# Joining the two first products of every table multiplication, two more groups of idle matmuls and a new order of work, in a fused S4 convolution and GLU kernel

## The chip, the cores and the metric

The kernel runs on one core of a Trainium2 chip. The metric is the device time of one execution in microseconds; for the kernel before it is the median of three runs. A separate execution was recorded by the hardware profiler, and every row that is shown comes from it.

## What is computed

The input x has 2048 tokens of 512 channels. It is normalised over the channels without learned parameters (xn). Two branches read xn, and the output is the input plus both of them.

```
K   = einsum("dn,dnl,dn->dl", Cc, exp(dt*A*l), dt*Bc).real      # 128 complex modes a channel
y   = irfft(rfft(xn, 4096) * rfft(K, 4096))[:2048] + xn*Dskip    # a causal convolution a channel
glu = (sigmoid(xn @ w_gate) * (xn @ w_up)) @ w_down              # 512 -> 1792 -> 512
out = x + y + glu
```

## The kernel before

**The plan.** The kernel first describes its work as 979 steps. `pl.add` names a step's engine, its modelled cost, the steps that it depends on and the slots of buffer pools that it takes and gives back. The list `ORDER` then fixes the sequence in which all steps are emitted, so it fixes the order on every engine and on every queue of transfers. Each engine works through its own steps strictly in that order. Slots are given out in the order of `ORDER` too: a pool with fewer buffers forces a later step behind the one that frees a buffer. Lists of step numbers choose engines: `ON_DVE` (which copies run on VectorE, the others run on ScalarE), `ON_ACT` (whose layer norm statistics ScalarE takes) and `UEV` (for which units of the GLU the up projection is first copied out of PSUM by ScalarE).

**The GLU branch.** There are four groups of 512 tokens (g0 to g3), and 14 blocks of 128 hidden channels in each. One block is a gate projection (L1027, four matmuls of 512 columns), a sigmoid on ScalarE (L1036), an up projection (L1042, four matmuls), and a product on VectorE (L1057). For a unit in `UEV` ScalarE first copies the up projection into `us_sb` (L1053), and the product reads that; otherwise the product reads PSUM directly. The down projection (L1086) takes 14 matmuls for each 128 tokens. Matmul groups land in eight PSUM banks, which the pool `b` hands out.

**The convolution branch.** It is a transform along tokens, a product with the transform of K, and the transform back:

- The tokens are transformed in pairs of tiles (`fx2`, L680), copied out of PSUM and stored to `z_scr` in DRAM.
- The powers of exp(dt*A) are made by a ladder of eleven squarings (L652 on ScalarE, L661 and L663 on VectorE). Each rung is cast into the tables `W` by a DMA that GpSimd issues (L657).
- For each of four blocks of 128 channels (c = 0 to 3) two tables are built: G with 16 columns and H with 41 columns of complex numbers. Columns that are rungs are copied in from `W` (the "seeds", by `pl.copy`). The others come from `cmul`, a complex multiplication of n columns by one rung, and from `squares` (L771 on ScalarE, L776 and L777 on VectorE).
- `cmul` is two steps. Its step `f_a` forms two products on VectorE: L718 writes the columns times the real part of the rung into the table, L719 writes the columns times the imaginary part into a temporary buffer. Its step `f_b` then combines them with two more instructions (L723, L724). A block has ten such multiplications, of n = 1, 1, 2, 2, 4, 4, 4, 4, 7 and 8 columns; n columns are 256 n elements a partition for L718 and for L719, and 128 n for L723 and L724. The temporary buffer has two slots (the pool `tg`).
- When G and H of a block are done, TensorE multiplies them (`f_k`, L802, two halves of 64 small matmuls). ScalarE or VectorE copies the result out, `f_sel` (L823, L827) sorts it, and two copies leave it in `kT`.
- Four pairs of frequency units then run for each of two channel halves, blocks 0 and 1 first: loads from `z_scr` and of a constant E, the transform `fm` (L870), the kernel's transform `fk` (L886), products on VectorE (L891, L895, L902, L903), the transform `fv` or `fvs` (L919, L931) and a store. At the end L995 transforms back, and L1010 and L1106 add.

**G and H in memory.** G has two buffers, chosen by the parity of c, so the steps of G for block c wait for the matmuls of block c-2 (`gdep`). H has one, so the steps of H for block c wait for the matmuls of block c-1 (`hdep`):

```
G = at(OFF["G"] + 8 * KB * (c % 2), [NPR, 2, NGE, 2])
H = at(OFF["H"], [NPR, 2, NH, 2])
gdep = kgen.get(c - 2, [])
hdep = kgen.get(c - 1, [])
```

**The start.** TensorE begins with groups of idle matmuls on zeros (`keep_warm`, L516): one of nine and, by `WARM`, two of two. They share its order with the transposes of the first four normalised tiles (L561).

Of the kernel before, what the change touches and what calls it, by code (L numbers as in the profile page):

```python
# [10 lines left out]
BF = mybir.dt.bfloat16  # L11
# [18 lines left out]
CW = 128  # L30
# [19 lines left out]
WARM = (2, 2)  # L50
# [132 lines left out]
def _consts():  # L183
# [22 lines left out]
UEV = (5, 7, 8, 12, 13, 14, 16, 17, 19, 20, 21, 24, 25, 26, 27, 28, 30, 31, 32, 33, 34, 35, 36, 37, 38, 39, 40, 41, 43, 44, 46, 50, 51, 52, 53, 54,)  # L206
ON_DVE = (93, 94, 95, 107, 116, 191, 192, 367, 373, 486, 492, 501, 548, 590, 595, 598, 879,)
ON_ACT = (2, 8, 10, 11, 12,)
ORDER = [
# [114 lines left out]
def kernel(  # L324
# [21 lines left out]
    pl = _Plan(dict(b=NBK, hT=NHT, zs=4, zx=2, xx=4, es=3, kb=2, pp=2, vs=2, ot=3, tg=2, us=2, sq=2))  # L346
# [27 lines left out]
    us_sb = const.tile([128, 2, 512], BF, name="us_sb")  # L374
# [9 lines left out]
    NBIG = 118272  # L384
# [16 lines left out]
    for nm, sz in [("W1", 12 * KB), ("gc", 2 * KB), ("G", 16 * KB), ("H", 20992), ("tmp", 4 * KB), ("W0", 12 * KB),  # L401
                   ("xn", 16 * KB), ("lad", 16 * KB), ("kx", 8 * KB), ("zs", 4 * KB), ("pq", 2 * KB)]:
        OFF[nm] = o
        o += sz
# [4 lines left out]
    W = [at(OFF["W%d" % p], [12, 2, DW]) for p in range(NP)]  # L409
# [211 lines left out]
    wt = [at(o_, [NP, 2, DW], F32) for o_ in (lad0, lad0 + 4 * KB, lad0 + 8 * KB, OFF["kx"])]  # L621

    def f_w0():
        wd = lambda n: pt_[n].rearrange("p (w d) -> p w d", w=NP)
        V.tensor_tensor(out=wt[0][:, :, 0], in0=wd("rr"), in1=wd("sh"), op=ALU.mult)
        V.tensor_tensor(out=wt[0][:, :, 1], in0=wd("rr"), in1=wd("sn"), op=ALU.mult)
# [22 lines left out]
    for k in range(12):  # L649
# [5 lines left out]
        def f_cw(cur=cur, k=k):  # L655
            for p in range(NP):
                P.dma_start(out=W[p][:, k], in_=cur[:, p])  # L657
# [47 lines left out]
    TMP = dict(tg=[OFF["tmp"], OFF["lad"] + 12 * KB])  # L705

    def cmul(lo, outp, n, m, conj, buf, deps, prio):

        ne = n * NPR * 4
        wide = lambda v: v.rearrange("p r c k h -> p r c (k h)")  # L710
        mre = m[:, 0, :].rearrange("p (r h) -> p r h", h=2).unsqueeze(2).to_broadcast([128, NPR, 2 * n, 2])
        mim = m[:, 1, :].rearrange("p (r h) -> p r h", h=2).unsqueeze(2).to_broadcast([128, NPR, 2 * n, 2])
        sl = _Slot(buf)
        tb = lambda: at(TMP[buf][sl.idx], [2048])[:, 0:ne].rearrange(
            "p (r c k h) -> p r c k h", r=NPR, c=2, h=2)

        def f_a():
            V.tensor_tensor(out=wide(outp), in0=wide(lo), in1=mre, op=ALU.mult)  # L718
            V.tensor_tensor(out=wide(tb()), in0=wide(lo), in1=mim, op=ALU.mult)  # L719

        def f_b():
# [461 lines left out]
```

## Time and profile before

| what | value |
|---|---|
| median of 3 runs | 215.97 us (215.88 to 215.99) |
| the profiled execution | 216.53 us |
| its span, first to last instruction | 214.7 us |
| around the span | 1.83 us |
| instructions | 5758 |

The profile's page gives the busy time of each engine, a picture of the span in 40 slices, the chain of work that ended last, and groups of instructions by line. The views of the trace add stretches of time, waits by releaser, and single instructions in order of time. PE is TensorE, PEld its weight loads, DVE is VectorE, ACT is ScalarE, POOL is GpSimd. A duration runs from an instruction's start to its end; on TensorE and VectorE the next one often starts before that end, so the distance from start to start, called the interval here, is what an instruction costs its engine.

### The profile page before, as it was taken

What the parts mean: (1) busy time and instruction counts of PE and PEld (TensorE: products, weight loads), DVE (VectorE), ACT (ScalarE), POOL (GpSimd) and SP (SyncE); (2) the same over time, 40 slices, a digit from 0 to 9 for tenths busy, and PEclk for the clock granted to TensorE, in tenths of its full rate; (3) what the DMA queues carried; (4) which work ended last, traced back from release to release, by engine and by line L of the source; (5) the groups of instructions that cost most, each with busy time, mean ns of one, the idle gap of its engine ahead of it and who ended that gap; (6) DMA issues with size and microseconds to landing.
All of it is one profiled execution on the core that took longest, in us unless ns stands there. A gap on an engine that the chain in (4) does not pass through costs nothing.

```text
span 214.7 us, 5758 instructions
## 1 busy us (share of the span) xinstructions
PE 203.3 (95%) x2235; PEld 103.2 (48%) x2263; DVE 196.1 (91%) x425; ACT 175.8 (82%) x358; POOL 32.3 (15%) x66
## 2 busy tenths in 40 slices
PE   7799999999999999999999899999989999999993
PEld 2464443444444454445565464645635555444352
DVE  3899999999999999999999999999789989975682
ACT  3899999999999999888999999965569999825000
POOL 4229051351101400000000005000011000000200
PEclk9999999999999999999999999999999999999999
DMA  6999949665976857347544739716957997768843
GB/s 189 391 419 437 253 121 183 99 130 84 291 187 139 173 196 195 116 150 254 162 147 138 195 65 272 162 53 137 269 111 174 312 288 226 231 179 235 231 160 138
DMA packets 41613, 42.37 MB, mean 197 GB/s; under 512 B 8809, under 2 KB 35058, under 8 KB 41458
## 3 DMA queue, kind: packets, MB, share of 16 engines
q1 hardware_dynamic: 36642, 36.95, 54.8%
q0 software_dynamic: 4512, 4.73, 14.5%
q8 instruction: 18, 0.29, 0.6%
q10 hardware_dynamic: 432, 0.33, 0.5%
q14 instruction: 9, 0.07, 0.1%
HBM read 25.21 MB, written 12.07 MB: 174 GB/s over the span
## 4 chain that ended last, share of the span: by engine, by line
PE 48%; DVE 35%; ACT 9%; issue 3%; DMA 2%; SPq 0%; DVEq 0%; ACTq 0%
PE bank L1086 16%; PE bank L1042 9%; PE bank L1027 8%; PE bank L886 6%; DVE hT_sb L1057 5%; DVE big L719 5%; ACT big L293 5%; DVE big L718 5%; DVE big L723 3%; DVE big L724 3%; DVE big L600 3%; DMA big<-in_A_par_dram 2%; DVE stats L538 2%; PE bank L919 2%; PE bank L931 2%
## 5 line engine op out<-in xcount | busy, mean ns | idle before, releaser
L293 ACT ACTIVATE big<-bank 128x512 bf16<-128x512 f32 (+2 forms) x146 | 81.6, 660 | 8.7 <-PE bank L802 3.0
L1027 PE MATMUL bank<-xnT,wg_sb 128*128 128x512 bf16 (+1 forms) x230 | 52.6, 361 | 1.5 <-ACT us_sb L1053 0.3
L1042 PE MATMUL bank<-xnT,wu_sb 128*128 128x512 bf16 x216 | 52.3, 379 | 0.7 <-issue 0.2
L1086 PE MATMUL bank<-wd_sb,hT_sb 128*128 128x512 bf16 (+1 forms) x232 | 50.1, 367 | 1.6 <-issue 0.9
L1086 PEld LDWEIGHTS <-hT_sb 128*128 128x128 bf16 x238 | 22.5, 98 | 27.4 <-issue 3.8
L1036 ACT ACTIVATE hT_sb<-bank 128x512 bf16<-128x512 f32 x56 | 34.9, 671 | 0.3 <-PE bank L1027 0.2
L1027 PEld LDWEIGHTS <-wg_sb 128*128 128x128 bf16 x244 | 22.7, 98 | 23.3 <-issue 3.7
L1042 PEld LDWEIGHTS <-wu_sb 128*128 128x128 bf16 x224 | 21.2, 98 | 26.3 <-issue 2.3
L718 DVE TENSOR_TENSOR big<-big 128x1024 bf16<-128x1024 bf16 (+4 forms) x40 | 26.5, 664 | 0.2
L1053 ACT ACTIVATE us_sb<-bank 128x512 bf16<-128x512 f32 x36 | 23.6, 702 | 3.6 <-PE bank L1042 3.6
L719 DVE TENSOR_TENSOR big<-big 128x1024 bf16<-128x1024 bf16 (+4 forms) x40 | 26.3, 658 | 0.0
L891 DVE TENSOR_TENSOR big<-big 128x2048 bf16<-128x2048 bf16 x16 | 19.4, 1214 | 0.7 <-ACT big L293 0.5
L886 PE MATMUL bank<-big 128*128 128x256 bf16 x160 | 19.8, 273 | 0.0
L886 PEld LDWEIGHTS <-big 128*128 128x128 bf16 x160 | 15.3, 98 | 5.5 <-issue 2.0
L293 ACT ACTIVATE big<-big 128x256 bf16<-128x256 bf16 x34 | 17.7, 538 | 0.2 <-PE bank L802 0.2
L657 POOL DMA_DIRECT2D big<-big x24 | 13.1, 549 | 27.5 <-DVE big L663 15.2
L771 ACT ACTIVATE sq_sb<-big 128x256 bf16<-128x256 bf16 (+2 forms) x20 | 14.5, 740 | 2.4 <-DVE big L724 1.4
L723 DVE TENSOR_TENSOR big<-big 128x512 bf16<-128x512 bf16 (+4 forms) x40 | 16.3, 408 | 0.0
L724 DVE TENSOR_TENSOR big<-big 128x512 bf16<-128x512 bf16 (+4 forms) x40 | 16.3, 408 | 0.0
L1057 DVE TENSOR_TENSOR hT_sb<-hT_sb,us_sb 128x512 bf16<-128x512 bf16 x36 | 14.6, 414 | 1.3 <-ACT us_sb L1053 1.2
L1057 DVE TENSOR_TENSOR hT_sb<-hT_sb,bank 128x512 bf16<-128x512 bf16 x20 | 13.4, 680 | 0.2 <-PE bank L1042 0.2
L652 ACT ACTIVATE big<-big 128x1024 f32<-128x1024 f32 x11 | 12.2, 1112 | 0.2 <-DVE big L663 0.2
(98 smaller groups left out, 208.6 us busy)
## 6 DMA issues: line engine op xcount, KB each, us to landing
big<-c_E SPq DMA_DIRECT2D x16, 320.0 KB, 4.0
z_scr<-big SPq DMA_DIRECT2D x16, 256.0 KB, 3.0
big<-z_scr SPq DMA_DIRECT2D x16, 256.0 KB, 4.2
v_scr<-big SPq DMA_DIRECT2D x16, 256.0 KB, 3.1
big<-big POOLq DMA_DIRECT2D x24, 128.0 KB, 3.0
big<-in_A_u_dram SPq DMA_DIRECT2D x4, 512.0 KB, 13.0
big<-v_scr SPq DMA_DIRECT2D x4, 512.0 KB, 5.0
wu_sb<-in_B_w_up_dram SPq DMA_DIRECT2D x2, 896.0 KB, 11.8
```

The source lines that it names most:

```text
L293: nc.scalar.activation(out=get(out), in_=get(in_), func=ACT.Identity)
L718: V.tensor_tensor(out=wide(outp), in0=wide(lo), in1=mre, op=ALU.mult)
L719: V.tensor_tensor(out=wide(tb()), in0=wide(lo), in1=mim, op=ALU.mult)
L723: V.tensor_tensor(out=outp[:, :, 0], in0=outp[:, :, 0], in1=tb()[:, :, 1], op=opr)
L724: V.tensor_tensor(out=outp[:, :, 1], in0=outp[:, :, 1], in1=tb()[:, :, 0], op=opi)
L886: T.matmul(bank(sk[kt == NKT - 1])[:, DW * c:DW * c + DW], es()[:, c, kt, :], kT[p][:, kt, :], start=kt in (0, NKT - 1), stop=kt >= NKT - 2)
L1027: T.matmul(bank(sl)[:, c0:c1], w_at(w, CUT_G, kt, k), xnT[:, grp, kt, c0:c1], start=(kt == 0), stop=(kt == KT - 1))
L1036: S.activation(out=hT_sb[:, hs.idx, k % 2, :], in_=bank(sl), func=ACT.Sigmoid)
L1042: T.matmul(bank(sl), w_at(wu_sb, CUT_U, kt, k), xnT[:, grp, kt, :], start=(kt == 0), stop=(kt == KT - 1))
L1053: S.activation(out=us_sb[:, us.idx, :], in_=bank(sl), func=ACT.Identity)
L1057: V.tensor_tensor(out=h(), in0=h(), in1=us_sb[:, us.idx, :] if on else bank(sl), op=ALU.mult)
L1086: T.matmul(bank(po)[:, 0:c[1] - c[0]], hT_sb[:, hts[k // 2].idx, k % 2, jj * 128:(jj + 1) * 128], wd_sb[:, k, c[0]:c[1]], start=first and ...
```

## The change

- `cmul` issues one VectorE instruction for both first products. Its pattern has a leading dimension of two: the input columns are read twice, the rung's real and imaginary parts are read one after the other, and the outputs go to the table's columns and to temporary columns.
- For that, the temporary columns lie in each table's own rows (G grows by 8 columns, H by 7), and `W` holds the real and imaginary parts of a block of 128 channels side by side. The pool `tg` of two slots becomes one slot for each table (`tG`, `tH`).
- G has one buffer in place of two, and `gdep` names block c-1.
- `us_sb` has three slots in place of two.
- `WARM` has four groups of two idle matmuls in place of two, so there are 981 steps, and every step from number 22 on has a number higher by two.
- `UEV` has 39 units in place of 36, `ON_DVE` has 26 steps in place of 17, `ON_ACT` holds five other tiles, and `ORDER` is another sequence throughout.

```diff
-WARM = (2, 2)
+WARM = (2, 2, 2, 2)
...
-UEV = (5, 7, 8, 12, 13, 14, 16, 17, 19, 20, 21, 24, 25, 26, 27, 28, 30, 31, 32, 33, 34, 35, 36, 37, 38, 39, 40, 41, 43, 44, 46, 50, 51, 52, 53, 54,)
-ON_DVE = (93, 94, 95, 107, 116, 191, 192, 367, 373, 486, 492, 501, 548, 590, 595, 598, 879,)
-ON_ACT = (2, 8, 10, 11, 12,)
+UEV = (0, 1, 3, 4, 5, 8, 14, 17, 18, 20, 21, 22, 23, 24, 25, 26, 27, 28, 29, 30, 31, 32, 33, 34, 35, 36, 37, 38, 39, 40, 41, 43, 45, 46, 48, 50, 52, 53, 54,)
+ON_DVE = (28, 39, 95, 96, 97, 109, 118, 129, 133, 135, 181, 191, 192, 193, 196, 240, 289, 375, 391, 485, 486, 498, 504, 545, 560, 597,)
+ON_ACT = (3, 11, 12, 14, 15,)
...
-    pl = _Plan(dict(b=NBK, hT=NHT, zs=4, zx=2, xx=4, es=3, kb=2, pp=2, vs=2, ot=3, tg=2, us=2, sq=2))
+    pl = _Plan(dict(b=NBK, hT=NHT, zs=4, zx=2, xx=4, es=3, kb=2, pp=2, vs=2, ot=3, tG=1, tH=1, us=3, sq=2))
...
-    W = [at(OFF["W%d" % p], [12, 2, DW]) for p in range(NP)]
+    W = [at(OFF["W%d" % p], [12, 2, 2, CW]) for p in range(NP)]
...
-    def cmul(lo, outp, n, m, conj, buf, deps, prio):
+    def cmul(tab, l0, o0, n, m, conj, buf, deps, prio):
...
+        flat = lambda v, lead: bass.AP(v.tensor, v.offset, [list(v.ap[0]), lead, [v.ap[2][0], 2 * NPR], [1, 2 * n]])
+        lo, outp, tb = wide(l0), wide(o0), wide(ext)
...
+        mall = bass.AP(m.tensor, m.offset, [list(m.ap[0]), [2, 2 * NPR], [0, 2 * n], [1, 2]])
...
         def f_a():
-            V.tensor_tensor(out=wide(outp), in0=wide(lo), in1=mre, op=ALU.mult)
-            V.tensor_tensor(out=wide(tb()), in0=wide(lo), in1=mim, op=ALU.mult)
+            V.tensor_tensor(out=flat(outp, [tb.offset - outp.offset, 2]), in0=flat(lo, [0, 2]), in1=mall, op=ALU.mult)
...
-        G = at(OFF["G"] + 8 * KB * (c % 2), [NPR, 2, NGE, 2])
-        H = at(OFF["H"], [NPR, 2, NH, 2])
-        gdep = kgen.get(c - 2, [])
+        G = at(OFF["G"], [NPR, 2, NGE + 8, 2])
+        H = at(OFF["H"], [NPR, 2, NH + 7, 2])
+        gdep = kgen.get(c - 1, [])
```

More of the change, by code (lines that the diff above doesn't have):

```diff
@@ L373 @@
     hT_sb = const.tile([128, NHT, 2, 512], BF, name="hT_sb")
-    us_sb = const.tile([128, 2, 512], BF, name="us_sb")
+    us_sb = const.tile([128, 3, 512], BF, name="us_sb")
     glu_sb = const.tile([128, 8, D], BF, name="glu_sb")
@@ L383 @@
     k2 = const.tile([128, 2 * KT], F32, name="k2")
-    NBIG = 118272
+    NBIG = 115200
     big = const.tile([128, NBIG // 2], BF, name="big")
@@ L400 @@
     OFF = {}
-    for nm, sz in [("W1", 12 * KB), ("gc", 2 * KB), ("G", 16 * KB), ("H", 20992), ("tmp", 4 * KB), ("W0", 12 * KB),
+    for nm, sz in [("W1", 12 * KB), ("gc", 2 * KB), ("G", 12 * KB), ("H", 24 * KB), ("tmp", 3 * KB // 2), ("W0", 12 * KB),
                    ("xn", 16 * KB), ("lad", 16 * KB), ("kx", 8 * KB), ("zs", 4 * KB), ("pq", 2 * KB)]:
@@ L620 @@
     lad0 = OFF["lad"]
-    wt = [at(o_, [NP, 2, DW], F32) for o_ in (lad0, lad0 + 4 * KB, lad0 + 8 * KB, OFF["kx"])]
+    wt = [at(o_, [2 * NP, 2, CW], F32) for o_ in (lad0, lad0 + 4 * KB, lad0 + 8 * KB, OFF["kx"])]
     def f_w0():
-        wd = lambda n: pt_[n].rearrange("p (w d) -> p w d", w=NP)
+        wd = lambda n: pt_[n].rearrange("p (w d) -> p w d", w=2 * NP)
         V.tensor_tensor(out=wt[0][:, :, 0], in0=wd("rr"), in1=wd("sh"), op=ALU.mult)
@@ L656, in f_cw @@
             for p in range(NP):
-                P.dma_start(out=W[p][:, k], in_=cur[:, p])
+                P.dma_start(out=W[p][:, k], in_=cur[:, 2 * p:2 * p + 2])
         c_op = pl.add("POOL", 1.0, f_cw, [cur_op], PLAD + k * 0.01 + 0.005, dma=(512 * KB, _rate(1024), 1.0))
@@ L704 @@
     w_use, g_use = [[], []], [[], []]
-    TMP = dict(tg=[OFF["tmp"], OFF["lad"] + 12 * KB])
-    def cmul(lo, outp, n, m, conj, buf, deps, prio):
[L709 to L712, printed above, removed]
+    def cmul(tab, l0, o0, n, m, conj, buf, deps, prio):
+        ext = NGE if buf == "tG" else NH
+        wide = lambda k0: tab[:, :, :, k0:k0 + n, :].rearrange("p r c k h -> p r c (k h)")
+        flat = lambda v, lead: bass.AP(v.tensor, v.offset, [list(v.ap[0]), lead, [v.ap[2][0], 2 * NPR], [1, 2 * n]])
+        lo, outp, tb = wide(l0), wide(o0), wide(ext)
+        assert list(outp.ap[1]) == [2 * outp.ap[2][0], NPR] and list(m.ap[1]) == [2 * NPR, 2]
+        mall = bass.AP(m.tensor, m.offset, [list(m.ap[0]), [2, 2 * NPR], [0, 2 * n], [1, 2]])
         sl = _Slot(buf)
-        tb = lambda: at(TMP[buf][sl.idx], [2048])[:, 0:ne].rearrange(
-            "p (r c k h) -> p r c k h", r=NPR, c=2, h=2)
         def f_a():
-            V.tensor_tensor(out=wide(outp), in0=wide(lo), in1=mre, op=ALU.mult)
-            V.tensor_tensor(out=wide(tb()), in0=wide(lo), in1=mim, op=ALU.mult)
+            V.tensor_tensor(out=flat(outp, [tb.offset - outp.offset, 2]), in0=flat(lo, [0, 2]), in1=mall, op=ALU.mult)
         def f_b():
             opr, opi = (ALU.add, ALU.subtract) if conj else (ALU.subtract, ALU.add)
-            V.tensor_tensor(out=outp[:, :, 0], in0=outp[:, :, 0], in1=tb()[:, :, 1], op=opr)
-            V.tensor_tensor(out=outp[:, :, 1], in0=outp[:, :, 1], in1=tb()[:, :, 0], op=opi)
-        a = pl.add("DVE", 0.135 + 0.269 * n, f_a, deps, prio, acq=[sl])
+            V.tensor_tensor(out=outp[:, :, 0], in0=outp[:, :, 0], in1=tb[:, :, 1], op=opr)
+            V.tensor_tensor(out=outp[:, :, 1], in0=outp[:, :, 1], in1=tb[:, :, 0], op=opi)
+        a = pl.add("DVE", 0.07 + 0.269 * n, f_a, deps, prio, acq=[sl])
         return pl.add("DVE", {1: 0.36, 2: 0.42, 4: 0.69, 7: 1.09}.get(n, 0.15 + 0.134 * n), f_b, [a], prio - 0.1, rel=[sl])
@@ L744 @@
             for q in range(0, n, st):
-                last = cmul(G[:, :, :, q:q + st, :], G[:, :, :, n + q:n + q + st, :], st, W[c // 2][:, 4 + lev, :, ws],
-                            True, "tg", [last, W_op[4 + lev]], PC)
+                last = cmul(G, q, n + q, st, W[c // 2][:, 4 + lev, c % 2], True, "tG", [last, W_op[4 + lev]], PC)
             n *= 2
@@ L756 @@
             seeds[dst] = pl.copy(nc, 0.31, H[:, :, :, dst, :].rearrange("p r c h -> p c r h"),
-                                 W[c // 2][:, src, :, ws].rearrange("p c (r h) -> p c r h", h=2), [W_op[src], w0_op, qb] + hdep, PC)
+                                 W[c // 2][:, src, c % 2].rearrange("p c (r h) -> p c r h", h=2), [W_op[src], w0_op, qb] + hdep, PC)
         h_ops = {}
@@ L763, in powers @@
         def powers(o0, l0, nn, lev, need):
-            h_ops[str(o0)] = cmul(H[:, :, :, l0:l0 + nn, :], H[:, :, :, o0:o0 + nn, :], nn, W[c // 2][:, lev, :, ws], False, "tg",
+            h_ops[str(o0)] = cmul(H, l0, o0, nn, W[c // 2][:, lev, c % 2], False, "tH",
                                   dep(need) + [W_op[lev], o_g], PC - 0.5)
@@ L801, in f_k @@
                             r = 16 * t + y
-                            T.matmul(pk[32 * t:32 * t + 32, y % 4, :], G[:, r, comp], H[:, r, comp],
+                            T.matmul(pk[32 * t:32 * t + 32, y % 4, :], G[:, r, comp, 0:NGE], H[:, r, comp, 0:NH],
                                      start=(comp == 0), stop=(comp == 1), tile_position=(0, 32 * t))
```

84 rows, old and new, of the table ORDER are left out of this document.

## The prediction

> **What bounds the kernel now.** I read the page's shares first, then busy time by stage, then the chain of work that ended last.
>
> ```profile
> PE 203.3 (95%) x2235; PEld 103.2 (48%) x2263; DVE 196.1 (91%) x425; ACT 175.8 (82%) x358; POOL 32.3 (15%) x66
> ```
>
> ```profile
> 25.00:65.00 40.00, 38.80 (x198) 16.86 (x202) 39.76 (x97) 39.55 (x81) 11.90 (x21) 1.00 0.74 156
> 65.00:113.00 48.00, 47.06 (x640) 23.32 (x644) 47.83 (x117) 45.88 (x101) 3.62 (x9) 1.00 0.60 172
> 113.00:150.70 37.70, 36.40 (x565) 20.38 (x572) 37.63 (x80) 33.45 (x73) 3.02 (x5) 1.00 0.57 146
> 150.70:214.70 64.00, 58.86 (x716) 31.02 (x726) 50.50 (x89) 36.01 (x72) 3.29 (x4) 1.00 0.74 212
> ```
>
> The columns are the stretch, its length, then PE, PEld, DVE, ACT and POOL busy. Up to 150.7 us VectorE has no hole: 47.83 of 48.00 and 37.63 of 37.70. TensorE is nearly full too. After 150.7 only TensorE is (58.86 of 64.00).
>
> ```profile
> 65.28 0.70 DVE big L718
> 65.98 0.60 DVE big L719
> ...
> 109.04 0.49 DVE big L724
> ...
> 150.68 1.52 PE bank L802 x128
> ...
> 156.93 0.91 issue
> ...
> 183.83 1.73 PE bank L1027 x8
> ```
>
> The chain runs over VectorE's table steps through the middle (first and last row of that stretch) and over TensorE at the end. 150.68 is the place that matters: there TensorE multiplies the last block's tables. Up to it the waits say who leads:
>
> ```profile
> PEld L1086 <- DVE hT_sb L1057: 1.2, 2, 1.0
> PEld L802 <- DVE big L723: 0.8, 2, 0.4
> PEld L802 <- DVE big L724: 0.5, 1, 0.5
> PEld L823 <- DVE big L291: 0.4, 1, 0.4
> ```
>
> TensorE's table matmuls (L802) waited for the last table additions in three of the four blocks. So up to 150.7 us the time is VectorE's work; from there to 214.7 it is TensorE's work plus its losses. My sum has these two halves.
>
> **VectorE up to the last table.** What does a merged instruction save? Two intervals against one:
>
> ```profile
> 74.28 0.68 DVE L718 TENSOR_TENSOR big<-big 128x1024 bf16<-128x1024 bf16 x1
> 74.88 0.68 DVE L719 TENSOR_TENSOR big<-big 128x1024 bf16<-128x1024 bf16 x1
> 75.48 0.41 DVE L1057 TENSOR_TENSOR hT_sb<-hT_sb,us_sb 128x512 bf16<-128x512 bf16 x1
> ...
> 76.83 1.21 DVE L718 TENSOR_TENSOR big<-big 128x2048 bf16<-128x2048 bf16 x1
> 77.97 1.21 DVE L719 TENSOR_TENSOR big<-big 128x2048 bf16<-128x2048 bf16 x1
> ```
>
> Two of 1024 take 75.48 - 74.28 = 1.20 from start to start; one of 2048 takes 77.97 - 76.83 = 1.14. Joining saves 0.067 us (the line through 0.60 and 1.14). By durations it would be 2 x 0.68 - 1.21 = 0.15, the upper bound, since only start-to-start time costs the engine. Below stands nothing, or a loss if the pattern with three free dimensions runs slower; the nearest row speaks against that, because L891 also rereads an input through a broadcast dimension and takes the same 1.21:
>
> ```profile
> L891 DVE TENSOR_TENSOR big<-big 128x2048 bf16<-128x2048 bf16 x16 | 19.4, 1214 | 0.7 <-ACT big L293 0.5
> ```
>
> I take 0.067. All forty multiplications lie ahead of the last table in both orders: 40 x 0.067 = 2.68 us less.
>
> The Trainium skill, page "VectorE: DVE Perf Modes", section "Side-by-side: where the cycles go for N=2048 bf16", gives each operation a fixed cost of about 158 cycles at 0.96 GHz. Forty joins would by that be worth an estimated 6.6 us. Its 1224 ns for 2048 elements agrees with the duration of 1214 here, but the interval of 1.14 does not carry that fixed cost, so the trace decides for 2.7.
>
> What does the new order put in place? I counted the VectorE steps of each kind that stand ahead of block 3's last table addition in the two sequences. Equal in both: the multiplications and squares, eleven statistics, the ladder, nine normalisations, and the unit products of six units. Different:
>
> - copies of 256 elements (seeds): 2 before, 7 after;
> - evictions of 512 from PSUM (two transposed tiles, three of the early transforms, one of U0.0): 0 before, 6 after;
> - GLU products from `us_sb`: 28 before, 31 after; from PSUM: 14 before, 12 after.
>
> ```profile
> 33.24 0.42 DVE L1057 TENSOR_TENSOR hT_sb<-hT_sb,us_sb 128x512 bf16<-128x512 bf16 x1
> 33.58 0.68 DVE L1057 TENSOR_TENSOR hT_sb<-hT_sb,bank 128x512 bf16<-128x512 bf16 x1
> 34.18 0.68 DVE L661 SCALAR_TENSOR_TENSOR big<-big 128x512 f32<-128x512 f32 x1
> ...
> 47.69 0.27 DVE L291 COPY big<-big 128x256 bf16<-128x256 bf16 x1
> 47.82 0.36 DVE L718 TENSOR_TENSOR big<-big 128x256 bf16<-128x256 bf16 x1
> ```
>
> Intervals: 0.34 from `us_sb`, 0.60 from PSUM (taken for the evictions too), 0.13 for a small copy. So 5 x 0.13 + 6 x 0.60 + 3 x 0.34 - 2 x 0.60 = 0.67 + 3.61 - 0.19 = 4.09 us more (unrounded intervals). Against 2.68 less, **the last table comes 1.40 us later on VectorE.** What the joins save is spent on taking eleven copies from ScalarE, which gets three copies of up projections instead; ScalarE was not in the way after 113 us (33.45 of 37.70), so that buys little.
>
> **TensorE after it.** Ahead of block 3's table matmuls the new order has 85 whole gate and up groups where the old has 83, the same 11 down projections, four `fm`, eight `fk`, three `fv`. A group costs 1.73 / 2 = 0.865 (row 183.83). So **1.73 us less is left behind that point.** The four idle matmuls are also ahead of it, where VectorE leads.
>
> ```profile
> 1.38 4.87 PE L516 MATMUL bank<-glu_sb 128*128 128x512 bf16 x11 [1.38 <-POOL glu_sb L502]
> 6.48 0.78 PE L516 MATMUL bank<-glu_sb 128*128 128x512 bf16 x2
> 7.41 0.40 PE L561 MATMUL bank<-ident,big 128*128 128x128 bf16 x4 [0.15 <-DVE big L552]
> 8.83 0.40 PE L561 MATMUL bank<-ident,big 128*128 128x128 bf16 x4 [1.02 <-DVE big L552]
> ```
>
> An idle group takes 0.78 or less, and TensorE idles 1.02 between transposes anyway: cover for one; the other is hidden as long as VectorE leads at the first tables, and costs up to 0.8 if not. The Trainium skill, page "TensorE: Matmul & The Clock Gate", section "Why this matters for your kernels", would have no idle gap beyond about 3 us. The gaps here are shorter and the rows after them run on at full pace, so by that rule the two groups buy nothing.
>
> **New waits.** G now waits for the matmuls of the block before. On VectorE's strict order everything behind the first step of block c waits with it. The table matmuls take 1.52 (row 150.68). Between a block's last addition and the next block's first step the new order has four GLU products (about 1.6 us) after block 0, two of them and an eviction (1.5) after block 1, and two unit products and two GLU products (2.4) after block 2. That just covers 1.52 if TensorE stands ready, and not if it comes late. Counted as above, TensorE now has 1.8 and 1.5 us more work ahead of the first two tables than VectorE has; before it had 0.5 and 0.6 less. Bounds: 0 and 3.3 us. But TensorE lost less time at the start:
>
> ```profile
> 3.60 0.69 DVE L538 BATCH_NORM_STATS2 stats<-big 128x6 f32<-128x512 bf16 x1 [3.60 <-DMA big<-in_A_u_dram]
> ```
>
> VectorE's first instruction came at 3.60, while TensorE's pauses up to 8.83 are 1.38 + 0.15 + 1.02 = 2.55. The difference of 1.05 leaves 0.75 and 0.45, and a wait of 0.75 at the first block sets VectorE back enough that the second vanishes: I take 0.7. One temporary slot for each table adds no wait: writer and reader are both VectorE, in order.
>
> The three slots of `us_sb` only loosen. wg's first piece is issued by ScalarE behind the first exponential, which waits for A_par:
>
> ```profile
> 1.24 0.46 ACTq L427 DMA_DIRECT2D wg_sb<-in_B_w_gate_dram  x1
> ...
> 7.09 0.63 ACT L598 ACTIVATE big<-big 128x512 bf16<-128x512 bf16 x1 [0.56 <-DMA big<-in_A_par_dram]
> ```
>
> It moves from 1.24 to about 7.6. The block k=0 that needs it stands behind k=2, k=1 and a second transform on TensorE, near 11.7; with the same flight (3.5) it lands near 11.1. I cost it at nothing; at worst 1 us, covered like the idle group. SP's queue sends the wide up weights earlier and x tiles 4 to 7 later, which suits the up projections that now come early.
>
> **After the last table.** The eviction that held L823 for 0.4 goes to ScalarE: 0.4 less. The 0.91 in the middle of a down projection has no releaser in the profile and belongs to no step; I let it go (bounds: 0.91 less, or again as much more). The unit transforms have about 0.8 to 1 us less distance behind their VectorE products than before: 0.4 more (bounds 0 and 1). The tail, from the last matmul on, is untouched.
>
> **Sum:** +1.40 - 1.73 + 0.7 - 0.4 - 0.91 + 0.4 = -0.54 us. Span 214.7 becomes 214.2; the profiled execution, 1.83 around it, 216.53 becomes 216.0. The median lies 0.56 under the profiled execution, so **215.4 us**.
>
> **Rivals.**
>
> - *The joins are worth their durations.* At 0.15 each the tables come 3.4 us earlier, and then TensorE is the bound: it can give back no more than the waits for VectorE listed (2.9) less the idle groups. 2.9 - 0.78 = 2.1 below my sum: 213.3. For it: VectorE leads everywhere up to 150.7. Against: the intervals. The fixed cost that the Trainium skill states on its page of VectorE would end here too, not at 6.6. The same end is reached if no boundary wait occurs and the unit waits vanish.
> - *Slower: one buffer for G.* If TensorE reaches a table more than about 0.1 us after VectorE finished it, VectorE stands idle for the difference, twice: up to 3.3, so 2.6 over my sum, 218.0; a middling 1.9 gives 216.6. For it: the counts of 1.8 and 1.5. Against: the 1.05 by which VectorE started later.
> - *The join saves nothing* (the wide pattern takes as long as two): 2.68 over, 218.1.
> - *No change:* the pause and the unit waits stay. 0.91 over my sum, 216.3.
>
> **Chances.** Forecast 0.40 (own range 214.7 to 216.1), early gain 0.22, one G buffer 0.23, no saving 0.07, no change 0.08. 0.2% is 0.43 us, about what a measurement can tell. Faster takes 0.34 of the forecast and the early gain: 0.56. Same takes 0.06 of the forecast and 0.06 of no change: 0.12. The rest, 0.32, is slower. For 8 in 10 the range takes in most of the early gain and of the G case: 213.2 to 217.6.
>
> **What would show it.** L718 alone, with 2048 elements at 1.14 from start to start where n is 4, forty times; VectorE without holes up to the last table except at block changes, where POOL's or ScalarE's releaser is L802; the last L802 near 152.8, and 61.4 us from there to the end. If the merged rows last longer than 1.21 the join failed; if VectorE idles over 1 us behind L802, the G case; if the last table stands before 151, the early gain.

## The result and the profile after

The changed kernel takes 219.89 us (median of 4 runs; one of them, 223.8, was disturbed and is left out of the ratio), the kernel before 215.98 us beside it. The ratio is 1.018, 95% interval 1.016 to 1.020: slower by 3.9 us, where 0.6 us faster was forecast. The profiled execution took 219.95 us, its span is 217.9 us; 2.05 lie around it.

The page of the changed kernel, busy time and the chain by engine:

```profile
PE 203.6 (93%) x2243; PEld 102.9 (47%) x2267; DVE 198.8 (91%) x394; ACT 174.4 (80%) x352; POOL 32.9 (15%) x66
...
DVE 56%; PE 28%; ACT 7%; issue 4%; DMA 3%; DVEq 0%; ACTq 0%
```

VectorE has 31 instructions fewer (394 for 425), and yet it is busy for 2.7 us more (198.8 for 196.1) and holds 56% of the chain. The stretches of the changed kernel, cut at the last table matmul (stretch, length, then PE, PEld, DVE, ACT, POOL), and the row of the chain at which they are cut:

```profile
25.00:65.00 40.00, 38.96 (x189) 17.20 (x191) 39.62 (x88) 38.98 (x75) 14.64 (x25) 1.00 0.69 149
65.00:113.00 48.00, 45.60 (x628) 22.26 (x632) 47.80 (x101) 42.59 (x96) 5.23 (x12) 1.00 0.62 158
113.00:155.87 42.87, 40.15 (x592) 21.44 (x595) 42.77 (x80) 36.91 (x79) 4.40 (x6) 1.00 0.52 132
155.87:217.90 62.03, 57.30 (x706) 30.59 (x714) 48.64 (x85) 35.80 (x72) 3.36 (x4) 0.99 0.80 230
```

```profile
155.87 1.34 PE bank L799 x122
```

L799 is the old L802. VectorE is full up to it, as before, while TensorE, which was at 47.06 of 48.00 in the middle, has sunk to 45.60; at all four tables it waits for VectorE's last additions (L721 and L722 in the waits shown under a_old2). The last table comes at 155.87 in place of 150.68 (5.2 later; 2.1 was forecast). From there to the end it takes 62.0 in place of 64.0 (61.4 was forecast). So the miss lies ahead of the last table, on VectorE. The groups of the joined instruction (L717 stands for the old L718 and L719), by size:

```profile
L717 DVE TENSOR_TENSOR big<-big 128x2048 bf16<-128x2048 bf16 x16 | 20.8, 1303 | 0.1
L717 DVE TENSOR_TENSOR big<-big 128x4096 bf16<-128x4096 bf16 x4 | 9.2, 2290 | 0.0
L717 DVE TENSOR_TENSOR big<-big 128x3584 bf16<-128x3584 bf16 x4 | 8.1, 2025 | 0.0
...
L717 DVE TENSOR_TENSOR big<-big 128x1024 bf16<-128x1024 bf16 x8 | 6.7, 834 | 0.0
...
L717 DVE TENSOR_TENSOR big<-big 128x512 bf16<-128x512 bf16 x8 | 5.4, 711 | 0.1
```

The 16 rows of 2048 elements last 1303 ns on average, where the same number of elements in one old product lasted 1210. By intervals it is plainer. VectorE's instructions in order of time, a multiplication of n=1 in each table and one of n=2 in H:

```profile
100.08 1.32 DVE L717 TENSOR_TENSOR big<-big 128x512 bf16<-128x512 bf16 x2
101.32 0.26 DVE L721 TENSOR_TENSOR big<-big 128x128 bf16<-128x128 bf16 x1
...
102.03 0.85 DVE L717 TENSOR_TENSOR big<-big 128x1024 bf16<-128x1024 bf16 x1
102.81 0.25 DVE L773 TENSOR_TENSOR big<-sq_sb 128x128 bf16<-128x128 bf16 x1
```

102.81 - 102.03 = 0.78 for n=2 in H, where the pair took 0.71 before and 0.71 - 0.067 = 0.64 would have been the forecast. The two of n=1 take 101.32 - 100.08 = 1.24. Summed over all forty, the intervals are 46.8 us before and 46.7 after: **the joins saved 0.1 us of the 2.68 forecast.** The pattern repeats in all four blocks: n=7 and n=8, and n=4 in G, cost about 0.067 less than the pair, as forecast, and n=1 in H falls at least as much (0.60 to 0.52); n=4 in H costs what the pair cost (1.204 before, 1.206 now, twelve times); n=2 in both tables, and n=1 in G, cost more than the pair.

### The profile page after: what moved, and what is told of

Read it like the earlier page. It is cut to its first block, busy times and chain, and to the rows that moved or that the text cites. A ratio compares the mean times of both kernels' runs of the same rounds, so it can differ in the third digit from the quotient of the medians.

```text
span 217.9 us, 5728 instructions
## 1 busy us (share of the span) xinstructions
PE 203.6 (93%) x2243; PEld 102.9 (47%) x2267; DVE 198.8 (91%) x394; ACT 174.4 (80%) x352; POOL 32.9 (15%) x66
## 3 DMA queue, kind: packets, MB, share of 16 engines
q0 software_dynamic: 4512, 4.73, 13.9%
## 4 chain that ended last, share of the span: by engine, by line
DVE 56%; PE 28%; ACT 7%; issue 4%; DMA 3%; DVEq 0%; ACTq 0%
DVE big L717 18%; PE bank L883 6%; DVE hT_sb L1054 6%; PE bank L1024 6%; DVE big L722 5%; PE bank L1039 5%; DVE big L721 5%; PE bank L1083 4%; ACT big L293 3%; DVE big L661 3%; DVE stats L538 3%; DVE big L663 3%; PE bank L928 2%; DMA out_dram<-big 2%; DVE big L888 2%
## 5 line engine op out<-in xcount | busy, mean ns | idle before, releaser
L293 ACT ACTIVATE big<-bank 128x512 bf16<-128x512 f32 (+2 forms) x144 | 75.0, 604 | 6.2 <-PE bank L799 2.1
L717 DVE TENSOR_TENSOR big<-big 128x2048 bf16<-128x2048 bf16 (+4 forms) x40 | 49.8, 1262 | 0.2
L1033 ACT ACTIVATE hT_sb<-bank 128x512 bf16<-128x512 f32 x56 | 33.3, 648 | 0.4 <-PE bank L1024 0.3
L768 ACT ACTIVATE sq_sb<-big 128x256 bf16<-128x256 bf16 (+2 forms) x20 | 13.2, 661 | 6.5 <-DVE big L722 5.1
L721 DVE TENSOR_TENSOR big<-big 128x512 bf16<-128x512 bf16 (+4 forms) x40 | 17.0, 424 | 0.1
L722 DVE TENSOR_TENSOR big<-big 128x512 bf16<-128x512 bf16 (+4 forms) x40 | 17.0, 425 | 0.0
L1054 DVE TENSOR_TENSOR hT_sb<-hT_sb,us_sb 128x512 bf16<-128x512 bf16 x39 | 15.9, 424 | 0.1
L1054 DVE TENSOR_TENSOR hT_sb<-hT_sb,bank 128x512 bf16<-128x512 bf16 x17 | 11.6, 682 | 2.3 <-PE bank L1039 2.2
L293 ACT ACTIVATE big<-big 128x256 bf16<-128x256 bf16 x29 | 12.4, 446 | 0.9 <-PE bank L799 0.9
L538 DVE BATCH_NORM_STATS2 stats<-big 128x6 f32<-128x512 bf16 x11 | 7.6, 687 | 3.8 <-DMA big<-in_A_u_dram 3.8
```

The costliest lines, as they stand in the source:

```text
L293: nc.scalar.activation(out=get(out), in_=get(in_), func=ACT.Identity)
L717: V.tensor_tensor(out=flat(outp, [tb.offset - outp.offset, 2]), in0=flat(lo, [0, 2]), in1=mall, op=ALU.mult)
L721: V.tensor_tensor(out=outp[:, :, 0], in0=outp[:, :, 0], in1=tb[:, :, 1], op=opr)
L722: V.tensor_tensor(out=outp[:, :, 1], in0=outp[:, :, 1], in1=tb[:, :, 0], op=opi)
L1033: S.activation(out=hT_sb[:, hs.idx, k % 2, :], in_=bank(sl), func=ACT.Sigmoid)
L1054: V.tensor_tensor(out=h(), in0=h(), in1=us_sb[:, us.idx, :] if on else bank(sl), op=ALU.mult)
```

## The experiments

Each kernel was timed in five rounds beside the kernel before (a_shift in one round). The medians of before were 215.6 to 216.2. "Intervals" are distances from start to start on VectorE, summed over the first products, and the median of the four blocks for one multiplication. The theories: **L**, the layout that the join needs takes back what the join saves; **W**, the joined pattern itself is slow; **V**, VectorE's work up to the last table is the time; **S**, ScalarE leads as well.

**a_split: the join undone in the new layout.**

```diff
-            V.tensor_tensor(out=flat(outp, [tb.offset - outp.offset, 2]), in0=flat(lo, [0, 2]), in1=mall, op=ALU.mult)
+            for comp, o_ in ((0, outp), (1, tb)):
+                mc = bass.AP(m.tensor, m.offset + comp * 2 * NPR, [list(m.ap[0]), [2, NPR], [0, 2 * n], [1, 2]])
+                V.tensor_tensor(out=o_, in0=lo, in1=mc, op=ALU.mult)
```

> The changed kernel with the two first products of a table multiplication issued as two instructions again; memory layout, order and everything else as changed. Theory L (the new layout takes back what joining saves: columns in short strided rows and temporary columns that start at odd byte offsets): in this layout too a pair costs one fixed 0.067 us more than the joined instruction, so 40 x 0.067 = 2.7 us more on VectorE ahead of the last table, 222.5 us, with L717-type pairs of n=2 near 0.85 (G 0.76). Theory W (the joined pattern itself runs slower than two narrow ones): the pairs fall back to the intervals of before (0.577, 0.686, 1.205 for n=1, 2, 4), the sum stays 46.8 us, and the time stays 219.9 within 0.3.

222.33 us, ratio 1.031 (1.028 to 1.034): 2.4 over the changed kernel. Its intervals sum to 49.0. So a join does save 49.0 - 46.7 = 2.3 us, and the layout costs 49.0 - 46.8 = 2.2. The groups of the two-instruction version, half of each group writing the table and half the temporary columns:

```profile
L719 DVE TENSOR_TENSOR big<-big 128x1024 bf16<-128x1024 bf16 x32 | 22.0, 733 | 0.1
...
L719 DVE TENSOR_TENSOR big<-big 128x512 bf16<-128x512 bf16 x16 | 6.9, 498 | 0.0
L719 DVE TENSOR_TENSOR big<-big 128x256 bf16<-128x256 bf16 x16 | 5.8, 425 | 0.1
```

733, 498 and 425 ns stand against 680 to 684, 423 to 429 and 360 to 377 before, for the same elements. L holds, W falls. The single intervals (median of the four blocks) show where: in H's first n=4 the product that goes to the table takes 0.599, the one that goes to the temporary columns 0.674; in H with n=2 it is the other way round, 0.445 and 0.341.

**a_old1: the old tables in the new order, one G buffer.** Old `cmul`, temporary pool and W; `G = at(OFF["G"], [NPR, 2, NGE, 2])`, `gdep = kgen.get(c - 1, [])`.

> The changed kernel with the old tables: two separate first products, contiguous temporary buffers (two slots), the old layout of W; one G buffer (rows of 16 columns) and the new order, engine lists and idle matmuls as changed. Theory (joins with the new layout saved 46.79 - 46.68 = 0.1 us in all): 219.9 within 0.4, and the whole loss of 3.9 us is that of the order and the engine lists. Rival (the join did save 2.7 us and the order costs 6.6): 222.6.

219.44 us, ratio 1.017 (1.014 to 1.020), the same as the changed kernel within the intervals. The joins with their layout are worth nothing; the whole loss is that of the rest of the change, the order and the engine lists above all.

**a_old2: as a_old1, with two G buffers.**

```diff
-        G = at(OFF["G"], [NPR, 2, NGE, 2])
-        gdep = kgen.get(c - 1, [])
+        G = at(OFF["G"] + 8 * KB * (c % 2), [NPR, 2, NGE, 2])
+        gdep = kgen.get(c - 2, [])
```

> As the one before it, with two G buffers as in the kernel before; order unchanged. If the single G buffer makes VectorE wait at the block boundaries as the prediction took it (0.7 us, bounds 0 and 3.3): 0.7 us under the kernel with one buffer, 219.2, with the waits for L799 gone. If the order put enough work between (covered): the same within 0.3.

220.41 us, ratio 1.020 (1.016 to 1.024); its runs scatter from 218.8 to 222.9. No gain is seen, so the single G buffer does not cost what the prediction booked for it. In the changed kernel's waits VectorE has none for the table matmuls; ScalarE has some, and TensorE stands ready at every table and waits for VectorE (seven waits), so it does not come late:

```profile
ACT big L293 <- PE bank L799: 3.0, 3, 2.1
PEld L799 <- DVE big L721: 1.9, 3, 1.0
PEld L799 <- DVE big L722: 1.4, 4, 0.8
```

**a_align: other places for the temporary columns.**

```diff
-        ext = NGE if buf == "tG" else NH
+        ext = {1: 18, 2: 18, 4: 16, 8: 16}[n] if buf == "tG" else {1: 44, 2: 44, 4: 44, 7: 41}[n]
```

> The changed kernel with the temporary columns at other places within the same rows: H from column 44 (176 bytes from the row's start) in place of 41 (164 bytes) for n = 1, 2 and 4; G from column 18 (72 bytes) in place of 16 (64 bytes) for n = 1 and 2. Theory L (offset of the temporary columns): joined rows of H with n=4 fall from 1.206 to 1.138 and those of n=2 from 0.785 to 0.62 (12 x 0.067 + 4 x 0.165 = 1.5 us), 218.4 us; G with n=1 and 2 tells whether its 64 bytes matter (4 x 0.187 + 4 x 0.078 = 1.1 us more if they fall, to 217.3). Rival W (the pattern or the row's length sets it, not the place): intervals unchanged, 219.9.

219.07 us, ratio 1.014 (1.012 to 1.017). H with n=4 falls from 1.207 to 1.135 with nothing changed but the byte at which its temporary columns start (176 for 164); the others stay. That H with n=2 stays at 0.785 was not expected; its run in the table itself starts at byte 12, and a_shift moves that one. The time lies halfway between the two that were expected. The group of 2048 elements is back at 1214 ns:

```profile
L717 DVE TENSOR_TENSOR big<-big 128x2048 bf16<-128x2048 bf16 x16 | 19.4, 1214 | 0.1
```

**a_fix: as a_align for H, and rows of G 128 bytes long** (`NGE + 16` in place of `NGE + 8`, G's temporary columns at 16).

> The changed kernel with rows of G 128 bytes long in place of 96 and H's temporary columns from 44 on: order, lists, one G buffer and idle matmuls as changed. Theory L (rows of 96 bytes cost G's n=1 and 2): these fall from 0.697 to 0.51 and 0.62, so with H's n=4 the joins save 0.84 + 4 x (0.187 + 0.078) = 1.9 us, the last table near 153.7, 218.0 us: what the joins of the change are worth with a layout that does not take them back, and still slower than before by the order. If only 64-byte rows do it: 219.0.

218.31 us, ratio 1.012 (1.009 to 1.015), as L expected. G with n=1 falls from 0.697 to 0.534 and with n=2 from 0.697 to 0.600. The intervals sum to 44.7, the last table matmul starts at 153.90. This is the change with 2.1 of the 2.7 us that were forecast for the joins, and it is still slower than before by 2.6. Beside the old tables in the same order (a_old1) it is 1.1 us faster.

**a_shift: as a_fix, with H's columns moved by 4 bytes.**

```diff
-        H = at(OFF["H"], [NPR, 2, NH + 7, 2])
+        H = at(OFF["H"], [NPR, 2, NH + 7, 2])[:, :, :, 1:]
```

> As a_fix, with all columns of H moved by one (4 bytes) in rows of the same 192 bytes; the temporary columns stay at byte 176 (for n=7 they lie in columns not yet filled). Theory B (what costs is a written run that crosses a 16-byte boundary in every row): H's n=2 now writes bytes 16 to 24 and falls from 0.785 to 0.62; H's n=4 now writes bytes 52 to 68, 116 to 132 and 148 to 164 and rises from 1.136 to about 1.205; n=1 unchanged (12 to 16); G unchanged; the time within 0.5 of 218.3. Rival (not the boundary but the place within the table, or the row's length): n=2 stays at 0.78 and n=4 at 1.136.

n=2 falls from 0.785 to 0.602 and n=4 rises from 1.136 to 1.225, both as theory B has it; 218.24 us. The groups of a_fix first, then of a_shift:

```profile
L717 DVE TENSOR_TENSOR big<-big 128x2048 bf16<-128x2048 bf16 x16 | 19.5, 1219 | 0.1
...
L717 DVE TENSOR_TENSOR big<-big 128x1024 bf16<-128x1024 bf16 x8 | 6.3, 784 | 0.0
```

```profile
L717 DVE TENSOR_TENSOR big<-big 128x2048 bf16<-128x2048 bf16 x16 | 20.7, 1294 | 0.1
...
L717 DVE TENSOR_TENSOR big<-big 128x1024 bf16<-128x1024 bf16 x8 | 5.6, 695 | 0.0
```

**b_dve: the old kernel, with the change's copies on VectorE.** The order, tables and buffers of before; only `ON_DVE` gains the six evictions and six seeds (26, 37, 127, 131, 133, 179, 189, 190, 194, 238, 287, 389) and loses one seed (192).

> The kernel before, order and tables untouched, with the twelve copies on VectorE that the change had given to it ahead of the last table, and the seed that it had taken away on ScalarE: 6 x 0.60 + 5 x 0.13 = 4.25 us more on VectorE in the old order, the same off ScalarE. Theory V (VectorE's work up to the last table is the time, ScalarE is not in the way): the last table near 154.5 in place of 150.7, and 219 to 220.2 us. Rival (ScalarE leads as well, so what it is spared comes back): 216 to 217.5.

219.87 us, ratio 1.018 (1.015 to 1.020): 4.2 slower, with nothing changed but who copies. The chain of waits has the last table matmul here:

```profile
154.78 1.35 PE bank L802 x126
```

154.78 - 150.68 = 4.1, against 4.25 priced (by VectorE's intervals its work up to there grew by 3.9). Theory V holds in the old order: work given to VectorE ahead of the last table is paid in full, and ScalarE's relief pays nothing back.

**a_back: these copies back on ScalarE in the new order** (`ON_DVE` of the changed kernel without 28, 39, 129, 133, 135, 181, 191, 192, 196, 240, 289, 391 and with 194).

> The changed kernel with twelve copies that the change had given to VectorE ahead of the last table back on ScalarE, and the one seed that it had taken away back on VectorE (the engine list of before, as far as the last table); all else as changed. The prediction priced these at 6 x 0.60 + 5 x 0.13 = 4.3 us of VectorE. Theory V (VectorE leads up to the last table, so its work is the time): the last table matmul comes up to 4 us earlier, 151.5 to 152.5 in place of 155.5, and the time is 215.9 to 217. Theory S (ScalarE, full early on, becomes late with them, so the order needed them there): the gain is eaten, 219 or more, with VectorE waiting for ScalarE.

221.91 us, ratio 1.029 (1.026 to 1.031): slower still, and theory V alone does not stand here. Up to its last table addition VectorE is busy for 4.0 us less than in the changed kernel (146.0 for 150.0), but this addition comes 2.1 later (157.85 for 155.74): VectorE now waits for ScalarE. From the waits of a_back, and its stretch from 5 to 25 us, with that of the changed kernel behind it:

```profile
DVE big L625 <- ACT big L617: 3.3, 1, 3.3
...
DVE big L717 <- ACT big L293: 1.9, 2, 1.3
```

```profile
5.00:25.00 20.00, 15.87 (x115) 9.01 (x115) 14.94 (x34) 19.11 (x34) 2.71 (x5) 1.00 1.02 398
```

```profile
5.00:25.00 20.00, 17.97 (x125) 10.09 (x126) 18.80 (x42) 18.16 (x33) 3.16 (x5) 1.00 1.03 396
```

VectorE does 14.94 us of work there in place of 18.80. It waits for the last step of the sines at the ladder's start (L617). ScalarE is full (19.11 of 20), but it was as full in the kernel before (19.16), so fullness alone is not the cause. What differs is the order. In the kernel before no copy of the first transforms (L293, from a bank into `big`) stands ahead of the sines on ScalarE; in the changed kernel five do, in a_back seven. L617 in the kernel before, the changed kernel and a_back:

```profile
13.94 0.72 ACT L617 ACTIVATE big<-big,one 128x512 f32<-128x512 f32 x1
...
16.23 0.72 ACT L617 ACTIVATE big<-big,one 128x512 f32<-128x512 f32 x1
...
17.26 0.72 ACT L617 ACTIVATE big<-big,one 128x512 f32<-128x512 f32 x1
```

So the new order cannot simply hand the copies back: what it puts ahead of the sines on ScalarE makes the ladder late unless VectorE takes part of it.

**a_late: only the five later copies back** (192, 196, 240, 289, 391 taken out of `ON_DVE`).

> As the one before it, but only the five copies from the second half of the table work on go back to ScalarE (four seeds of 0.13 and one eviction of 0.60: 1.14 us of VectorE). Theory V: 218.8. Theory S: 219.9 within 0.3.

220.06 us, ratio 1.022 (1.019 to 1.024): the 1.14 us taken off VectorE do not show. It speaks for S again. In its trace, as in a_back's (the second wait shown there, 1.9), VectorE waits 2.0 us in the second and third block at H's first multiplication (L717) for a copy on ScalarE (L293), a wait that the changed kernel does not have; the seed that this multiplication reads is among those handed back. That this wait took the 1.14 us is likely, not shown.

**a_nowarm: the two added groups of idle matmuls empty** (`WARM = (0, 2, 0, 2)`).

> The changed kernel with the two added groups of idle matmuls empty again (four matmuls of 0.216 us less); order and all else as changed. The prediction took them as covered: 219.9 within 0.3, granted clock unchanged. Rival (TensorE is late at the first table, so they count): 0.4 to 0.86 less, 219.0 to 219.5. Rival (they keep the clock up): slower, with a lower clock at the start.

220.85 us, ratio 1.024 (1.019 to 1.028), runs from 219.3 to 222.6. No gain, so the groups do not cost the loss. The granted clock is 1.000 in its profiled run, so there is no sign that they were needed either. The scatter does not allow a finer statement.

**b_join: the join alone in the old order, temporary columns in columns not yet filled** (`TJ = {2: 28, 3: 30, 12: 28, 17: 33, 28: 36}`, G from column 8; rows as long as before).

> The kernel before, order and engine lists and both G buffers untouched, with 31 of its 40 pairs of first products joined; the temporary columns lie in columns of the same table that are not filled yet, so that the rows keep their old lengths (64 bytes in G, 164 in H); W as in the changed kernel. Theory L (a join is worth 0.067 us where the layout stays): 31 x 0.067 = 2.1 us less on VectorE, the last table near 148.7, and the time 214.0 to 215.1, 214.5 as a middle. Rival (joins are worth nothing in any layout): 215.9 within 0.3. Rival (worth their durations, 0.15): 212.5 to 213.5.

226.57 us, ratio 1.048 (1.044 to 1.052). This run says nothing on the join. Its instructions wait for each other where those of before did not: five copies on ScalarE wait 4.7 us for the joined product, where no copy waited for the products before, and VectorE waits in its turn:

```profile
DVE big L722 <- ACT big L293: 4.5, 3, 2.3
...
DVE big L722 <- ACT sq_sb L777: 2.4, 2, 1.8
```

L722 is the joined product there. In the old order seeds and squares lie between the products, and the columns that they read or write lie between a product's own columns and its temporary ones; that the added waits come from this range is argued, not shown.

**b_join2: the join in the old order without such waits.** 36 joins; H in rows of 192 bytes with temporary columns from 44 on, G in rows of 64 with columns 8 to 15; two steps of `ORDER` moved.

> The kernel before with its engine lists and both G buffers, and 36 of its 40 pairs joined (all but G's n=8). G's temporary columns are columns 8 to 15 of the same rows, which stay 64 bytes long; H's rows are 192 bytes as in the changed kernel, with the temporary columns from 44 on (41 for n=7). Two steps of ORDER move: the second half of c1.pA12 and of c3.pA12 comes ahead of the next multiplication of H. One temporary buffer for G's n=8; no added waits of VectorE for ScalarE or the other way round. Theory L: G's n=1, 2 and H's n=4 now come out at 0.51, 0.62 and 1.135, only H's n=2 (out at byte 12) stays at 0.78; 36 x 0.067 - 4 x 0.165 = 1.75 us less on VectorE, the last table near 149, and 214.2 to 215.2 us. Rival (a join is worth nothing to the time, since TensorE takes over): 215.6 to 215.9.

217.42 us, ratio 1.007 (1.004 to 1.009): not faster but 1.8 slower, although its joined products have the intervals that were expected (0.50 and 0.60 in G, 1.135 for n=4 in H, 0.79 for n=2).

**b_split2: b_join2 with its 36 joins undone.**

> The kernel b_join2 (old order with two steps moved, rows of H 192 bytes, temporary columns in the tables, one temporary buffer) with its 36 joined pairs issued as two instructions again: everything but the join is the same. b_join2 took 217.4 us where before took 215.7, and its joined rows saved about 1.3 us of VectorE while VectorE's idle time rose by 2.0 us (0.88 for POOL, 0.46 and 0.76 for ScalarE). If a join is worth 0.067 us to the time once the layout is fixed: 36 x 0.067 = 2.4 us more, 219.8, and layout and moved steps, not the join, are what costs b_join2 its gain. If the waits for POOL and ScalarE take what a join saves (VectorE comes earlier to steps that are not ready): 217.4 within 0.4, with those waits smaller.

216.85 us, ratio 1.005 (1.002 to 1.007). That is 0.15 below the range expected for the waits, and far from 219.8. The two intervals overlap: in the old order no gain of the join is seen. Its work is saved: the intervals of the first products sum to 47.8 with two instructions, of which 0.65 are idle time, so 47.2; joined to 47.0, of which 1.55 are idle time, so 45.4. Up to the last table addition VectorE is busy for 1.3 us less in b_join2 (144.9 for 146.3) and idle for 1.4 more between its first step and there, and the addition comes no earlier (152.1 for 151.7). VectorE's waits in b_join2 are these:

```profile
DVE ln_nb L488 <- POOL ln_ri L484: 0.9, 1, 0.9
...
DVE big L715 <- ACT sq_sb L770: 0.8, 1, 0.8
...
DVE big L775 <- ACT sq_sb L770: 0.5, 1, 0.5
```

and b_split2 has only one like them, of 0.4:

```profile
DVE big L776 <- ACT sq_sb L771: 0.4, 1, 0.4
```

VectorE comes earlier to steps for which POOL or ScalarE is not ready. What b_split2 loses against before (1.0) goes with layout, moved steps and the single temporary buffer, which no run takes apart: up to the last table addition VectorE is busy for 0.7 us more there than before, 0.4 of it in the first products (47.2 for 46.7), and idle for 0.7 more, and it starts 0.35 earlier.

No version that was run beats the kernel before.

## Why the prediction was wrong

- **What bounds the kernel: right.** VectorE up to the last table, TensorE behind it. b_dve shows it directly: steps priced at 4.25 us, put on VectorE, moved the last table by 4.1 and the time by 4.2.
- **"Joining saves 0.067 us ... 40 x 0.067 = 2.68 us less": this step failed.** 0.1 us came of it. The rate itself was right: a_split pays 2.3 us for undoing the joins. What failed is the sentence that the nearest row (L891) speaks against a loss. That row has long runs; it says nothing on rows with runs of 4 to 16 bytes. The change lays the tables out anew for the join, and that layout costs 2.2 us on the same instructions. The sign that the prediction named for this came: the merged rows of 2048 elements last 1303 ns on average, over 1.21. The rival "the join saves nothing", given 0.07, came true in its saving alone: its reason (the wide pattern itself takes as long as two) is refuted by a_split, and its 218.1 is 1.8 below what was measured.
- **Not priced at all: the second half of a multiplication.** The additions run in the new rows too. Those of 256 elements lasted 301 and 284 ns before (L723, L724) and last 336 now (L721, L722). By intervals all additions took 0.57 us more, and the squares, which stand in the same rows, 0.33 less:

```profile
L722 DVE TENSOR_TENSOR big<-big 128x256 bf16<-128x256 bf16 x8 | 2.7, 336 | 0.0
L721 DVE TENSOR_TENSOR big<-big 128x256 bf16<-128x256 bf16 x8 | 2.7, 336 | 0.0
```

- **Copies and evictions moved to VectorE, +4.09: right in size, in part by luck** (b_dve: 4.1 for the copies). By intervals they and the GLU products took 4.2 more in the changed kernel. Two errors cancel in it: the two transposed tiles took 0.34 each in place of 0.60, and two of the seven seeds 0.49 and 0.56 in place of 0.13. That the relief of ScalarE "buys little" holds in the old order; a_back shows that in the new order VectorE must have these copies.
- **Waits from one G buffer, +0.7: not found.** a_old2 gains nothing from the second buffer, and the trace has no wait of L717 for L799. TensorE did not come late to the tables, as this term supposed. That about as much was lost otherwise is luck: VectorE's first instruction starts 0.2 later, and its idle time from there to the last table addition is 0.45 longer.
- **Idle matmuls at nothing: not contradicted** (a_nowarm).
- **After the last table, -2.64 forecast, -1.97 measured.** TensorE's busy time there falls by 58.86 - 57.30 = 1.56 (1.73 forecast); the time in which it is not busy falls from 5.14 to 4.73, by 0.4 in place of 0.9. That the 0.91 pause would be gone and little else take its place was the weaker part.

The sum again, by what was measured: the last table later by 3.09 than forecast (2.6 from the joins, 0.57 - 0.33 from additions and squares, the other terms within 0.15 each), the rest longer by 0.67. -0.54 + 3.09 + 0.67 = +3.2, the difference of the spans (217.9 - 214.7). Around the span lie 2.05 in place of 1.83, and the profiled run of before lay 0.56 above its median, that of after only 0.06; with 0.2 and 0.5 that makes 3.9 between the medians.

## What to carry to other kernels

A merged instruction is priced by rows that have its own row length, its own run length and its own start byte; where the merge needs a new layout, every instruction that touches the layout is priced anew. On the engine that leads, count the work that an order hands to it: that term was right, and larger than the saving. And a saving on the leading engine is worth its size only where what it comes to next is ready: in the new order 40 joins took 2.3 us off VectorE's products and 2.4 off the time, in the old order 36 took off 1.7 and none of the time.

## What the runs showed of the hardware

In these runs VectorE's product of bfloat16 columns cost more when written runs of 8 or 16 bytes crossed a 16-byte boundary in every row. In the 192-byte rows of a_split, 8-byte runs that start at byte 12 took 0.445 per 512 elements, at byte 164 (no crossing) 0.341; 16-byte runs took 0.674 per 1024 elements at byte 164 (crossing) and 0.599 at byte 48. Moving all columns by 4 bytes swapped the two (a_shift: 0.785 to 0.602, and 1.136 to 1.225). In the old 164-byte rows, whose start moves by 4 bytes from row to row, little of it is seen (0.355 for the 8-byte runs at byte 12, 0.60 for the 16-byte ones), although three of four 16-byte runs cross there. Runs of 28 bytes show none of it: joined, they took 1.935 in a_fix, where each lies in two such stretches of 16 bytes, and 1.935 in a_shift, where each lies in three. So the crossing alone does not set the cost. Read runs that cross, as those of H's first n=4 at byte 4, show no cost (1.132 in a_align).

Rows of 96 bytes are slow in another way: runs of 4 and of 8 bytes took the same 0.37 there, where rows of 64 took 0.28 and 0.335; joined, 0.697 for both, against 0.534 and 0.600 in rows of 128. No boundary of 16 bytes is crossed in these; why the row's length matters is open.
